# Two stacks of four heads' outputs used in turn, and the four steps that finish a stack moved to later units, in a one-core adaLN block with windowed attention

## The chip, the cores and the metric

The kernel runs on one core of a Trainium2 chip. Its time is the device time of one execution in microseconds (us); three executions were timed, and the median of the three is the metric. One more execution was profiled. Engines are named as in the profile: PE (TensorE, matmuls), PEld (its weight loads), DVE (VectorE), ACT (ScalarE), POOL (GpSimd), SP (SyncE, which issues nearly all DMAs, strictly one after the other).

## The reference

```python
h = _layernorm(x) * (1 + ca) + sa                       # x: 2048 x 448
q, k, v = split(h @ wqkv)                               # 16 heads of 28
scores = einsum("bhqd,bhkd->bhqk", q, k) * 28 ** -0.5
mask = (idx[:, None] - idx[None, :] >= 0) & (idx[:, None] - idx[None, :] < 256)
p = softmax(where(mask, scores, -1e9))
x = x + ga * (einsum("bhqk,bhkd->bhqd", p, v) @ wo)
h = _layernorm(x) * (1 + cb) + sb
x = x + gb * (mish(h @ w1 + b1) @ w2)                   # 448 -> 1792 -> 448
```

sa, ca, ga, sb, cb, gb are rows made of a condition vector; all is float32.

## The kernel before

The 2048 rows are four groups of 512 (g = 0 to 3). Each group has 16 heads, so attention is 64 heads ("slots") i = 16g + h, and each slot is three **units** u = 3i, 3i+1, 3i+2, the three blocks of keys that its 512 queries see. Matmul operands are split into a high and a low part (hi, lo) to keep the precision, which is why there are two or three matmuls for each product.

The order of the work is written out by hand in one loop over u (the loop with `for u in range(NU + 9)`). In the iteration of unit u, with s = u // 3 and k = u % 3, it records, in this order:

- `PV(u - 4, Pl)`: the low part of the probabilities of unit u-4 times the values, into the PSUM tile pv of its slot (line 750). At k = 0 also `EV(s - 2)`, which copies the finished pv of slot s-2 to the staging tile O2 (ACT, line 756).
- `B(u)`: the scores with keys on the partitions (PE, tile sB, line 718), the mask by a matmul (line 729), and two exponentials on ACT, P (line 732) and its rounded copy Ph (line 733). The row maximum is subtracted inside the matmul: two rows of the query tile q hold it.
- `SP(u - 1)`: the low piece Pl = P - Ph of the unit before (POOL, line 740, one subtraction of 128x512).
- `A(s + 3, t)`: for a slot three ahead, scores with queries on the partitions (PE, tile sA, line 688) and their row maximum with the mask (DVE, tile junk, line 690). Two PSUM buffers serve all sA.
- a load of q and k for a later slot from the scratch tensor scr (SP); then the filler of the group: matmuls of the projections qk and qk_v and of the output projection wo (line 323), as many as a credit of RATE per unit allows, with their evictions.
- `M2`: every six units the row maxima of two slots are transposed on PE (line 696), split on DVE (mr, lines 698 and 699) and sent by two small DMAs into the q tiles (q<-mr). `B` of the first of these slots, three units later, reads them.
- At k = 1 `EM(s - 2)`: two DMAs move the staged output of a slot to its place in a stack of four heads: rows 0 to 31 of the staging tile to partitions 32(i % 4) and on of tile O4 (o<-o), rows 32 to 59 to the same partitions of tile OL4 (ol<-o). O4 holds the product with the high part of the values and the row sum of the softmax, OL4 the product with the low part. `PV(u - 2, Ph)` ends the iteration.

There is one pair O4, OL4. When its four heads are in, **four steps** finish the stack of quad qd (slots 4qd to 4qd+3):

- `QA(qd)`: on = O4 + OL4, POOL, line 776;
- `T1(qd)`: a transpose by 32x32 blocks into T4 and a reciprocal of the row sums, DVE, lines 782 and 784;
- `TM(qd)`: T4 times the reciprocals, POOL, line 789;
- `T2(qd)`: the transpose back, DVE, line 793. The last quad of a group then sets `on_full`, for which that group's output projection (gen_oT and gen_wo, in the next group's filler) waits.

Before the change QA stands at the very start of unit 12qd+18, ahead of that unit's `SP`; T1 in unit 12qd+19, TM in 12qd+20, T2 in 12qd+22. The last transfer into the stack is recorded in unit 12qd+16, and the first into the same pair for the next quad in unit 12qd+19. Engines take their instructions in the recorded order, and a waiting instruction holds all that is behind it on its engine; a DMA that SP waits to issue holds the later ones. The last four slots don't use the staging tile: EV copies them straight into O4 and OL4 (lines 758 and 759), and the last quad's four steps are recorded together after the last unit. After attention (about 472 us) comes the dense part: z and acc matmuls (lines 937, 1130 to 1132).

Of the kernel before, what the change touches and what calls it, by code (L numbers as in the profile page):

```python
# [8 lines left out]
F32 = mybir.dt.float32  # L9
F32R = mybir.dt.float32r  # L10
BF16 = mybir.dt.bfloat16
AF = mybir.ActivationFunctionType
ALU = mybir.AluOpType

S, D, F, H, DH, W = 2048, 448, 1792, 16, 28, 256
NG, GT = 4, 512
# [35 lines left out]
def adaln_block(ctx: ExitStack, tc: tile.TileContext, x, wqkv, wo, w1, b1, w2, c, w_mod, out):  # L52
    nc = tc.nc
    PE, ACT, DVE, POOL = nc.tensor, nc.scalar, nc.vector, nc.gpsimd
# [3 lines left out]
    def dma(o, i):  # L58
        nc.sync.dma_start(o, i)

    def pool(name, side="left", space=None):
        kw = {} if space is None else {"space": space}
        cm = tc.tile_pool(name=name, bufs=1, reuse_waits="tile", side=side, **kw)
        st = ExitStack()
        return st.enter_context(cm), st
# [45 lines left out]
    for k in range(4):  # L111
        wmf = st0.tile([128, 2 * D], F32, name=f"wm01_{k}")
        t = wmf[0:112]
# [199 lines left out]
    def drain(*gs):  # L313
        for g in gs:
            for _ in g:
                pipe.step()
# [17 lines left out]
    def flush():  # L334
        while later:
            later.pop(0)()
# [185 lines left out]
    att, att_s = pool("att")  # L522
# [1 line left out]
    Q3 = [Q2[i // 2][:, i % 2] for i in range(NQ)]  # L524
    k3_tile(att, NK - 1)

    O4, OL4, T4, O2 = [att.tile([128, GT], F32, name=n) for n in ("o4", "ol4", "t4", "o2")]
    POOL.memset(OL4, 0.0)
    wo3 = [mid.tile([128, D], F32R, name=f"wo3_{i}", tag="wo", bufs=8) for i in range(4)]
    wol = [mid.tile([128, D], F32R, name=f"wol_{i}", tag="wo", bufs=8) for i in range(4)]  # L530

# [142 lines left out]
    NS = NG * H  # L674
    mx, Pt, Ph, Pl, pvb = {}, {}, {}, {}, {}
# [34 lines left out]
    def B(u):  # L710
        i, b = divmod(u, 3)
        g, h = divmod(i, H)
        q, k = Q3[i % NQ], K3[i % NK]
        bl = units(g, b)
        c0 = bl[0][3]
        p = bank("sB", 2, f"sB{u}")
        for n, (jj, t0, t1, c) in enumerate(by_width(bl)[::-1]):
            PE.matmul(p[:, c:c + 128 * (t1 - t0)], k[:, jj * 128:(jj + 1) * 128], q[:, t0 * 128:t1 * 128],  # L718
                      start=(n == 0), stop=False, skip_group_check=True)
        far = {c + 128 * (jj - t0) for jj, t0, t1, c in bl if t0 <= jj < t1}  # L720
        diag = {c + 128 * (jj - 2 - t0) for jj, t0, t1, c in bl if t0 <= jj - 2 < t1}
        masked = []
        for c in sorted(far | diag):
            if c in far:
                masked.append((256 if c + 128 in diag else 128, c, 0))
            elif c - 128 not in far:
                masked.append((128, c, 128))
        for n, c, m in sorted(masked):
            PE.matmul(p[:, c:c + n], identr, fdmask[:, m:m + n], start=False, stop=True, skip_group_check=True)  # L729
        P = Pt[u] = att.tile([128, 512], F32, name=f"P{u}", tag="P", bufs=4)  # L730
        Ph[u] = att.tile([128, 512], F32R, name=f"Ph{u}", tag="Ph", bufs=4)
        ACT.activation(P[:, c0:], p[:, c0:], AF.Exp, scale=SCALE)  # L732
        ACT.activation(Ph[u][:, c0:], p[:, c0:], AF.Exp, scale=SCALE)  # L733

    def SP(u):
        i, b = divmod(u, 3)
        c0 = units(i // H, b)[0][3]
        Pl[u] = att.tile([128, 512], F32R, name=f"Pl{u}", tag="Pl", bufs=4)
        for eng, a, b in ((POOL, c0, 512),) if u < NU - 5 else ((POOL, 0, 256), (DVE, 256, 512)):
            eng.tensor_tensor(Pl[u][:, a:b], Pt[u][:, a:b], Ph[u][:, a:b].bitcast(F32), op=ALU.subtract)  # L740

    def PV(u, P):
        i, b = divmod(u, 3)
        g, h = divmod(i, H)
        if P is Ph and b == 0:
            pvb[i] = bank("pv", 2, f"pv{i}")
        pv = pvb[i]
        for n, (jj, t0, t1, c) in enumerate(by_width(units(g, b))):
            j = 4 * g - 2 + jj
            PE.matmul(pv[0:60, t0 * 128:t1 * 128], V[j % NV][:, h, :], P[u][:, c:c + 128 * (t1 - t0)],  # L750
                      start=(P is Ph and b == 0 and n == 0), stop=False, skip_group_check=True)

    def EV(i):
        a, b = i % 4 * 32, i % 2 * 64
        if i < NS - 4:
            ACT.activation(O2[b:b + 60], pvb[i][0:60, :], AF.Copy)  # L756
        else:
            ACT.activation(O4[a:a + 32], pvb[i][0:32, :], AF.Copy)
            DVE.tensor_copy(OL4[a:a + DH], pvb[i][32:60, :])

    def EM(i):
        a, b = i % 4 * 32, i % 2 * 64
        if i < NS - 4:
            dma(O4[a:a + 32], O2[b:b + 32])
            dma(OL4[a:a + DH], O2[b + 32:b + 60])

    def quad(qd):
        g, ci = divmod(qd, 4)
        if ci == 0 and g not in on:
            on[g] = mid.tile([128, 4, GT], F32, name=f"on{g}", tag="on")  # L770
        return on[g][:, ci], T4.rearrange("p (b d) -> p b d", d=32)

    def QA(qd):
        o, t = quad(qd)
        for eng, a, b in ((POOL, 0, GT),) if qd < NS // 4 - 1 else ((POOL, 0, 192), (DVE, 192, GT)):
            eng.tensor_tensor(o[:, a:b], O4[:, a:b], OL4[:, a:b], op=ALU.add)

    rcq = {}

    def T1(qd):  # L780
        o, t = quad(qd)
        DVE.transpose(T4, o)
        rcq[qd] = att.tile([128, 16, 1], F32, name=f"rc{qd}", tag="rc", bufs=1)
        DVE.reciprocal(rcq[qd], t[:, :, 28:29])

    def TM(qd):
        o, t = quad(qd)
        for eng, a, b in ((POOL, 0, 16),) if qd < NS // 4 - 1 else ((POOL, 0, 6), (DVE, 6, 16)):
            eng.tensor_tensor(t[:, a:b, 0:28], t[:, a:b, 0:28], rcq[qd][:, a:b].to_broadcast([128, b - a, 28]), op=ALU.mult)

    def T2(qd):
        o, t = quad(qd)
        DVE.transpose(o, T4)
        if qd % 4 == 3:
            on_full.add(qd // 4)
# [213 lines left out]
    def step(g):  # L1009
        return next(fillers[g], 99.0) or RATE[g]  # L1010
# [40 lines left out]
    for u in range(NU + 9):  # L1051
        s, k = divmod(u, 3)
        g = s // H
        if k == 0 and s % H == 0 and 0 < g < NG:
            drain(fillers[g - 1], side[g - 1])
            flush()
        pipe.step()
        qd = (s - 6) // 4
        if s % 4 == 2 and 0 <= qd < NS // 4 - 1 and k == 0:
            QA(qd)  # L1060
        if 0 <= u - 4 < NU:
            PV(u - 4, Pl)
            if k == 0:
                EV(s - 2)
        if u < NU:
            B(u)
        if 0 <= u - 1 < NU:
            SP(u - 1)
        a = s + LEAD
        if a < NS:  # L1070
            A(a, (0, 1, 3)[k])
        if k == s % 2 and s < NS:
            load_slot(s + LEAD + 2)
        if 0 <= qd < NS // 4 - 1:
            if s % 4 == 2 and k == 1:
                T1(qd)
            if s % 4 == 2 and k == 2:
                TM(qd)
            if s % 4 == 3 and k == 1:
                T2(qd)  # L1080
        if k == 0 and s - 2 == NS - 1:
            for f in (QA, T1, TM, T2):
                f(NS // 4 - 1)
        if g < NG:
            v = u - 48 * g
            if v in (0, 12):
                chunk["v"] = 4 if v == 0 and g or 0 < g < NG - 1 else 2
            if v == 0:
                credit = 0.0
            credit += RATE[g] * (2 if v < FRONT[g] else 1)  # L1090
            while credit > 0.0:
                credit -= step(g)
        if k == 0 and (a - 1) % 2 == 1 and LEAD <= a - 1 < NS:
            M2((a - 1) // 2)
        if g < NG:
            if v > 1 or g == 0:
                side_step(g, ("dve", "act")[a >= NS:] if k == 1 else ("act",) if k == 0 and s % 2 == 0 else ())
            if later and ((s + (k == 2)) % 2 == 0 or k == 1):
# [12 lines left out]
        if 0 <= u - 2 < NU:  # L1111
            PV(u - 2, Ph)
# [53 lines left out]
    for n in range(NN + 1):  # L1166
        g, f = divmod(n, NF)
# [44 lines left out]
```

## Time and profile before

| | us |
|---|---|
| median of three timed executions (768.67, 770.18, 770.5) | 770.18 |
| the profiled execution | 768.72 |
| its span | 766.9 |
| PE busy in the span | 701.2 |
| DVE, ACT, POOL busy | 397.6, 392.1, 347.9 |
| mean granted clock of PE | 0.962 |

The span runs from the first to the last instruction of the program; the 1.8 us between it and the execution's time lie around it. A busy share is an average over stages, so what a change in attention is worth has to be read from the stretch of attention, about 59 to 472 us. PEclk is the share of the full TensorE clock that was granted: where it is 0.5, a matmul takes about twice as long. The idle time that a view puts ahead of an instruction is put down to the wait that ended last.

### The profile page before, as it was taken

What the parts mean: (1) busy time and instruction counts of PE and PEld (TensorE: products, weight loads), DVE (VectorE), ACT (ScalarE), POOL (GpSimd) and SP (SyncE); (2) the same over time, 40 slices, a digit from 0 to 9 for tenths busy, and PEclk for the clock granted to TensorE, in tenths of its full rate; (3) what the DMA queues carried; (4) which work ended last, traced back from release to release, by engine and by line L of the source; (5) the groups of instructions that cost most, each with busy time, mean ns of one, the idle gap of its engine ahead of it and who ended that gap; (6) DMA issues with size and microseconds to landing.
All of it is one profiled execution on the core that took longest, in us unless ns stands there. A gap on an engine that the chain in (4) does not pass through costs nothing.

```text
span 766.9 us, 11988 instructions
## 1 busy us (share of the span) xinstructions
PE 701.2 (91%) x3873; PEld 594.2 (77%) x3873; DVE 397.6 (52%) x993; ACT 392.1 (51%) x723; POOL 347.9 (45%) x363
## 2 busy tenths in 40 slices
PE   8999868969899979899987879999999999999996
PEld 8777656748778858787866768888888888888885
DVE  6676645667646657756575778443422232323112
ACT  4467645766746657756665679343323322322221
POOL 6545865678454678555586695642100000000002
PEclk9999998989989979999989899999999999999999
DMA  7856762364456364464667425530110020001001
GB/s 223 264 192 201 206 205 86 107 198 126 134 175 204 100 188 142 138 177 152 183 192 208 126 70 181 169 108 1 50 48 0 1 96 0 1 1 49 0 1 49
DMA packets 53730, 91.13 MB, mean 119 GB/s; under 512 B 8086, under 2 KB 28228, under 8 KB 53668
## 3 DMA queue, kind: packets, MB, share of 16 engines
q1 hardware_dynamic: 53204, 90.36, 38.5%
q8 instruction: 31, 0.51, 0.3%
q14 instruction: 31, 0.25, 0.1%
q10 hardware_dynamic: 464, 0.00, 0.0%
HBM read 53.34 MB, written 29.36 MB: 108 GB/s over the span
## 4 chain that ended last, share of the span: by engine, by line
PE 65%; issue 13%; DMA 8%; DVE 6%; POOL 3%; ACT 3%; SPq 1%; POOLq 0%; ACTq 0%; DVEq 0%
PE z L937 14%; PE pv L750 8%; PE qk L323 7%; PE wo L323 5%; PE sB L718 4%; PE acc L1132 4%; PE acc L1130 4%; PE acc L1131 4%; DMA ol<-o 4%; PE sA L688 4%; PE sB L729 3%; PE qk_v L323 2%; DVE junk L690 2%; POOL Pl L740 2%; PE warm L436 1%
## 5 line engine op out<-in xcount | busy, mean ns | idle before, releaser
L740 POOL TENSOR_TENSOR Pl<-P,Ph 128x512 fp32r<-128x512 f32 (+2 forms) x192 | 233.9, 1232 | 68.7 <-ACT Ph L733 45.9
L690 DVE CUSTOM_DVE_ANT_0 junk<-sA,mask 128x384 bf16<-128x384 f32 (+2 forms) x256 | 133.8, 523 | 93.3 <-PE sA L688 82.6
L732 ACT ACTIVATE P<-sB 128x512 f32<-128x512 f32 (+2 forms) x192 | 109.5, 570 | 81.6 <-PE sB L729 76.0
L945 DVE TENSOR_TENSOR al<-t,ah 128x512 fp32r<-128x512 f32 x56 | 40.8, 728 | 187.1 <-ACT ah L944 187.0
L943 ACT ACTIVATE t<-z,b1c 128x512 f32<-128x512 f32 x56 | 38.5, 687 | 190.0 <-PE z L937 183.2
L688 PE MATMUL sA<-k,q 84*128 84x384 f32 (+2 forms) x256 | 104.1, 416 | 7.5 <-DVE mx L690 6.2
L733 ACT ACTIVATE Ph<-sB 128x512 fp32r<-128x512 f32 (+2 forms) x192 | 109.2, 569 | 0.0
L750 PE MATMUL pv<-Pl,v 128*60 128x256 f32 (+2 forms) x352 | 79.0, 300 | 30.6 <-POOL Pl L740 30.5
L718 PE MATMUL sB<-q,k 86*128 86x256 f32 (+1 forms) x352 | 80.5, 304 | 14.2 <-DMA q<-mr 8.5
L937 PE MATMUL z<-hhf,w 128*128 128x512 f32 x224 | 89.5, 399 | 0.0
L937 PE MATMUL z<-hlf,w 128*128 128x512 f32 x224 | 88.5, 395 | 0.0
L750 PE MATMUL pv<-Ph,v 128*60 128x256 f32 (+2 forms) x352 | 82.1, 309 | 0.0
L1130 PE MATMUL acc<-w2h,ah 128*128 128x448 f32 x224 | 81.9, 366 | 0.0
L1132 PE MATMUL acc<-w2h,al 128*128 128x448 f32 x224 | 81.9, 366 | 0.0
L1131 PE MATMUL acc<-w2l,ah 128*128 128x448 f32 x224 | 81.5, 364 | 0.0
L718 PEld LDWEIGHTS sB<-q,k 86*128 86x128 f32 x352 | 65.4, 205 | 19.7 <-issue 8.8
L750 PEld LDWEIGHTS pv<-Pl,v 128*60 128x60 f32 x352 | 47.3, 141 | 42.3 <-POOL Pl L740 36.3
L937 PE MATMUL z<-hhf,w1l 128*128 128x512 f32 x168 | 66.4, 395 | 0.0
L688 PEld LDWEIGHTS sA<-k,q 84*128 84x128 f32 x256 | 51.9, 207 | 15.6 <-DVE mx L690 10.9
L729 PE MATMUL sB<-fdmask,identr 128*128 128x128 bf16 (+1 forms) x320 | 63.8, 267 | 0.0
L750 PEld LDWEIGHTS pv<-Ph,v 128*60 128x60 f32 x352 | 48.8, 142 | 13.8 <-issue 2.0
L756 ACT ACTIVATE o<-pv 60x512 f32<-60x512 f32 x60 | 35.3, 589 | 41.7 <-PE pv L750 39.2
(157 smaller groups left out, 1261.2 us busy)
## 6 DMA issues: line engine op xcount, KB each, us to landing
scr<-st SPq DMA_DIRECT2D x24, 512.0 KB
k<-scr SPq DMA_DIRECT2D x48, 252.0 KB
q<-scr SPq DMA_DIRECT2D x64, 168.0 KB
scr<-st SPq DMA_DIRECT2D x32, 256.0 KB
x<-x1d SPq DMA_DIRECT2D x10, 448.0 KB
o<-o SPq DMA_DIRECT2D x60, 64.0 KB
xin<-in_A_x_dram SPq DMA_DIRECT2D x8, 448.0 KB
xr<-in_A_x_dram SPq DMA_DIRECT2D x16, 224.0 KB
```

Of the source, the lines that this page charges most:

```text
L323: PE.matmul(p, b, a, start=(n == 0), stop=(n == len(ps) - 1))
L688: PE.matmul(p[:, c0:384], q[0:84, t * 128:(t + 1) * 128], k[0:84, t * 128 + c0:t * 128 + 384], start=True, stop=True)
L690: DVE.tensor_tensor_reduce(out=junk[:, c0:384], in0=p[:, c0:384], in1=mask[:, c0:384], scale=1.0, scalar=-3.0e38, op0=ALU.add, op1=ALU.max ...
L718: PE.matmul(p[:, c:c + 128 * (t1 - t0)], k[:, jj * 128:(jj + 1) * 128], q[:, t0 * 128:t1 * 128], start=(n == 0), stop=False, skip_group_ch ...
L732: ACT.activation(P[:, c0:], p[:, c0:], AF.Exp, scale=SCALE)
L733: ACT.activation(Ph[u][:, c0:], p[:, c0:], AF.Exp, scale=SCALE)
L740: eng.tensor_tensor(Pl[u][:, a:b], Pt[u][:, a:b], Ph[u][:, a:b].bitcast(F32), op=ALU.subtract)
L750: PE.matmul(pv[0:60, t0 * 128:t1 * 128], V[j % NV][:, h, :], P[u][:, c:c + 128 * (t1 - t0)], start=(P is Ph and b == 0 and n == 0), stop=F ...
L937: PE.matmul(zb[n], ps[m][1], ps[m][0], start=(m == 0), stop=(m == 10))
L1130: PE.matmul(p, ah[n][:, ts], w2h[f], start=(f == 0), stop=False)
L1131: PE.matmul(p, ah[n][:, ts], w2l[f], start=False, stop=False)
L1132: PE.matmul(p, al[n][:, ts], w2h[f], start=False, stop=(f == NF - 1))
```

## The change

O4 and OL4 become two pairs (two lists of two tiles); T4 and O2 keep their roles and get the names t4_0 and t4_1, so in rows of the changed program the staging tile reads "t". EV, EM and QA choose the pair by the quad's parity, i // 4 % 2. The four steps of a quad move to one unit each, in units 12qd+20 to 12qd+23, and behind that unit's `B`, `SP`, `A` and load instead of ahead of them. The last quad's steps stay where they are. One more memset clears the second OL4.

```diff
-    O4, OL4, T4, O2 = [att.tile([128, GT], F32, name=n) for n in ("o4", "ol4", "t4", "o2")]
-    POOL.memset(OL4, 0.0)
+    O4, OL4, (T4, O2) = [[att.tile([128, GT], F32, name=f"{n}_{i}") for i in range(2)] for n in ("o4", "ol4", "t4")]
+    for t in OL4:
+        POOL.memset(t, 0.0)
...
     def EM(i):
-        a, b = i % 4 * 32, i % 2 * 64
+        a, b, n = i % 4 * 32, i % 2 * 64, i // 4 % 2
         if i < NS - 4:
-            dma(O4[a:a + 32], O2[b:b + 32])
-            dma(OL4[a:a + DH], O2[b + 32:b + 60])
+            dma(O4[n][a:a + 32], O2[b:b + 32])
+            dma(OL4[n][a:a + DH], O2[b + 32:b + 60])
...
-            eng.tensor_tensor(o[:, a:b], O4[:, a:b], OL4[:, a:b], op=ALU.add)
+            eng.tensor_tensor(o[:, a:b], O4[qd % 2][:, a:b], OL4[qd % 2][:, a:b], op=ALU.add)
...
         pipe.step()
-        qd = (s - 6) // 4
-        if s % 4 == 2 and 0 <= qd < NS // 4 - 1 and k == 0:
-            QA(qd)
         if 0 <= u - 4 < NU:
             PV(u - 4, Pl)
...
         if k == s % 2 and s < NS:
             load_slot(s + LEAD + 2)
-        if 0 <= qd < NS // 4 - 1:
-            if s % 4 == 2 and k == 1:
-                T1(qd)
-            if s % 4 == 2 and k == 2:
-                TM(qd)
-            if s % 4 == 3 and k == 1:
-                T2(qd)
+        qd, w = divmod(u - 20, 12)
+        if 0 <= qd < NS // 4 - 1 and w < 4:
+            (QA, T1, TM, T2)[w](qd)
```

EV changes as EM does: for the last four slots it writes O4[n] and OL4[n].

Two places of the program's order are shown, both of quad 5 (the sixth). On POOL, the rows before (Pl are the low pieces of one unit each, on is the sum QA, t the multiplication TM):

```order
L740 TENSOR_TENSOR Pl_2694<-P_2663,Ph_2664 128x512
L776 TENSOR_TENSOR on_2358<-o_462,ol_463 128x512
L740 TENSOR_TENSOR Pl_2721<-P_2690,Ph_2691 128x512
L740 TENSOR_TENSOR Pl_2748<-P_2717,Ph_2718 128x512
L740 TENSOR_TENSOR Pl_2776<-P_2744,Ph_2745 128x512
L789 TENSOR_TENSOR t_464<-t_464,rc_2754 128x16x28
L740 TENSOR_TENSOR Pl_2803<-P_2772,Ph_2773 128x512
```

and the same stretch of POOL in the changed program (buffer numbers differ between the programs: the first three rows are the units of Pl_2721, Pl_2748 and Pl_2776 above):

```order
L741 TENSOR_TENSOR Pl_2717<-P_2691,Ph_2692 128x512
L741 TENSOR_TENSOR Pl_2742<-P_2713,Ph_2714 128x512
L741 TENSOR_TENSOR Pl_2773<-P_2738,Ph_2739 128x512
L777 TENSOR_TENSOR on_2426<-o_1_463,ol_1_465 128x512
L741 TENSOR_TENSOR Pl_2796<-P_2769,Ph_2770 128x512
L741 TENSOR_TENSOR Pl_2829<-P_2792,Ph_2793 128x512
L790 TENSOR_TENSOR t_0_466<-t_0_466,rc_2803 128x16x28
L741 TENSOR_TENSOR Pl_2911<-P_2825,Ph_2826 128x512
```

Three low pieces that stood behind the sum now stand ahead of it; between the sum and the multiplication there are two instead of three.

On DVE, before (the pairs L690 are the row maxima of one sA tile; L262 and L270 split a transposed tile; L698 and L699 make mr):

```order
L782 STREAM_TRANSPOSE t_464<-on_2358 128x512
L784 RECIPROCAL rc_2754<-t_464 128x16
L690 ISA junk,mx_2639<-sA_2_2758,mask 128x384
L690 ISA mx_2639 128x1
L262 TENSOR_SCALAR tr_2728<-tr_2728,cols 128x512
L270 TENSOR_TENSOR hl_2585<-tr_2728,hh_2584 128x512
L690 ISA junk,mx_2639<-sA_3_2778,mask 128x384
L690 ISA mx_2639 128x1
L690 ISA junk,mx_2805<-sA_0_2806,mask 128x384
L690 ISA mx_2805 128x1
L698 CAST mr_2814<-sA_3_2778 8x128
L699 TENSOR_TENSOR mr_2814<-sA_3_2778,mr_2814 8x128
```

and in the changed program:

```order
L691 ISA junk,mx_2639<-sA_3_2775,mask 128x384
L691 ISA mx_2639 128x1
L262 TENSOR_SCALAR tr_2747<-tr_2747,cols 128x512
L270 TENSOR_TENSOR hl_2611<-tr_2747,hh_2610 128x512
L691 ISA junk,mx_2798<-sA_0_2799,mask 128x384
L691 ISA mx_2798 128x1
L783 STREAM_TRANSPOSE t_0_466<-on_2426 128x512
L785 RECIPROCAL rc_2803<-t_0_466 128x16
L699 CAST mr_2811<-sA_3_2775 8x128
L700 TENSOR_TENSOR mr_2811<-sA_3_2775,mr_2811 8x128
```

The transpose T1 and its reciprocal have moved behind three row maxima and now stand directly ahead of the two instructions that make mr.

In groups 1 and 2, where the output projection waits for `on_full`, its first matmuls come one unit later and what follows them in the group's filler moves back by a unit; the order of the dense part is unchanged.

More of the change, by code (lines that the diff above doesn't have):

```diff
@@ L757, in EV @@
         else:
-            ACT.activation(O4[a:a + 32], pvb[i][0:32, :], AF.Copy)
-            DVE.tensor_copy(OL4[a:a + DH], pvb[i][32:60, :])
+            ACT.activation(O4[n][a:a + 32], pvb[i][0:32, :], AF.Copy)
+            DVE.tensor_copy(OL4[n][a:a + DH], pvb[i][32:60, :])
     def EM(i):
-        a, b = i % 4 * 32, i % 2 * 64
+        a, b, n = i % 4 * 32, i % 2 * 64, i // 4 % 2
         if i < NS - 4:
-            dma(O4[a:a + 32], O2[b:b + 32])
-            dma(OL4[a:a + DH], O2[b + 32:b + 60])
+            dma(O4[n][a:a + 32], O2[b:b + 32])
+            dma(OL4[n][a:a + DH], O2[b + 32:b + 60])
     def quad(qd):
```

## Prediction

> **What bounds the kernel now.** I read the page first, then the engines' busy time by stage, then PE's waits.
>
> ```profile
> span 766.9 us, 11988 instructions
> 59.00:160.00 101.00, 81.35 (x485) 63.95 (x484) 58.89 (x187) 60.40 (x130) 63.66 (x62) 0.95 0.53 164
> 160.00:272.00 112.00, 103.05 (x633) 87.69 (x632) 70.62 (x202) 72.41 (x135) 71.03 (x62) 0.93 0.50 150
> 272.00:385.00 113.00, 100.58 (x633) 85.78 (x633) 70.15 (x201) 72.43 (x135) 75.20 (x66) 0.95 0.55 166
> 385.00:460.00 75.00, 61.32 (x391) 50.34 (x391) 53.89 (x140) 50.04 (x96) 58.36 (x50) 0.91 0.50 146
> 460.00:767.00 307.00, 300.44 (x1418) 260.46 (x1417) 104.25 (x157) 104.10 (x168) 47.12 (x53) 0.99 0.15 47
> ```
>
> Each row is a stretch, its length, the busy time of PE, PEld, DVE, ACT and POOL, the granted clock, the DMA share and GB/s. From 460 us on PE is busy for 300.44 of 307 us; nothing here is to be had there. In the four rows of attention PE is busy for 346.3 of 401 us, so it idles 54.7 us, and no other engine comes near it: POOL, the next, has 268.3. What ends PE's waits:
>
> ```profile
> PE pv L750 <- POOL Pl L740: 30.5, 14, 4.3
> PE sB L718 <- DMA q<-mr: 8.5, 6, 3.7
> PE sA L688 <- DVE mx L690: 6.2, 12, 1.0
> PE sB L718 <- ACT Ph L733: 4.7, 5, 2.2
> ```
>
> (total us, times, longest.) More than half of the idle time is one wait: PV wants a low piece that POOL has not made. It comes 14 times, and there are 15 quads in the loop. POOL itself in attention:
>
> ```profile
> L740 POOL TENSOR_TENSOR Pl<-P,Ph 128x512 fp32r<-128x512 f32 x179 | 222.6, 1258 | 61.8 <-ACT Ph L733 40.4 <-PE sA L688 7.7 <-POOL Pl L740 4.9
> L776 POOL TENSOR_TENSOR on<-o,ol 128x512 f32<-128x512 f32 x15 | 19.1, 1273 | 70.6 <-DMA ol<-o 35.9 <-PE sA L688 18.5 <-DMA q<-scr 6.1
> L789 POOL TENSOR_TENSOR t<-t,rc 128x448 f32<-128x448 f32 x14 | 13.8, 983 | 0.0
> ```
>
> Ahead of 15 sums POOL idles 70.6 us, 4.7 us each. The views name several releasers, but the sum reads only the stack and waits for its transfers. Quad 5 shows the whole event:
>
> ```profile
> 201.18 0.28 DVE L699 TENSOR_TENSOR mr<-sA,mr 8x128 fp32r<-8x128 f32 x1
> 203.81 0.47 PE L718 MATMUL sB<-q,k 86*128 86x384 f32 x2
> 204.18 0.81 SPq L59 DMA_DIRECT2D ol<-o  x1
> 204.83 0.56 DVE L690 CUSTOM_DVE_ANT_0 junk<-sA,mask 128x384 bf16<-128x384 f32 x1
> 205.39 0.40 PE L718 MATMUL sB<-q,k 86*128 86x256 f32 x2
> 206.57 0.40 PE L718 MATMUL sB<-q,k 86*128 86x384 f32 x2
> 209.50 1.26 POOL L776 TENSOR_TENSOR on<-o,ol 128x512 f32<-128x512 f32 x1 [6.10 <-DMA ol<-o]
> 210.72 3.74 POOL L740 TENSOR_TENSOR Pl<-P,Ph 128x512 fp32r<-128x512 f32 x3
> 210.79 0.56 SPq L59 DMA_DIRECT2D o<-o  x1
> 210.80 0.71 DVE L782 STREAM_TRANSPOSE t<-on 128x512 f32<-128x512 f32 x1 [3.47 <-POOL on L776]
> 211.54 0.25 DVE L784 RECIPROCAL rc<-t 128x16 f32<-128x16 f32 x1
> 212.04 0.68 PE L750 MATMUL pv<-Pl,v 128*60 128x128 f32 x2 [3.06 <-POOL Pl L740]
> ```
>
> The last transfer is issued at 204.18 and the sum starts at 209.50, 5.3 us later. Three low pieces wait behind it, DVE's transpose waits for it (3.47 us), SP's next o<-o waits for it, and PE stands for 3.06 us. Units are 1.2 to 1.6 us long here (203.81, 205.39, 206.57).
>
> The clock follows. These stretches begin at PE's stalls behind a sum (the last one at the copy of the end of attention, below):
>
> ```profile
> 132.00:139.80 7.80, 7.07 (x36) 5.29 (x36) 6.30 (x19) 5.54 (x12) 7.80 (x8) 0.78 0.36 98
> 159.00:168.00 9.00, 7.40 (x39) 6.17 (x40) 5.36 (x18) 4.62 (x9) 8.68 (x11) 0.62 0.41 121
> 210.00:218.00 8.00, 5.96 (x23) 5.10 (x24) 4.79 (x13) 2.32 (x5) 7.83 (x7) 0.57 0.07 17
> 275.00:284.00 9.00, 7.07 (x31) 5.80 (x32) 5.17 (x18) 4.22 (x8) 8.68 (x11) 0.53 0.50 147
> 384.00:393.00 9.00, 7.08 (x31) 5.24 (x32) 5.85 (x16) 3.48 (x7) 8.54 (x8) 0.62 0.34 114
> 436.00:445.00 9.00, 7.88 (x39) 6.49 (x40) 7.62 (x20) 4.83 (x10) 8.83 (x9) 0.62 0.18 54
> 459.00:468.00 9.00, 9.00 (x53) 7.42 (x52) 7.67 (x14) 8.88 (x18) 5.55 (x7) 0.81 0.02 5
> ```
>
> Length times missing clock, summed over the seven, is 21.4 us; counting only what PE was busy, 17.6 us.
>
> **The change part by part.** The sum stood at the head of unit 12qd+18 and now comes behind the low piece of unit 12qd+19: three low pieces go ahead of it.
>
> *The low-piece waits, -30.5.* In quad 5 POOL's wait of 6.10 us is to be covered by three units, 3 x 1.5 = 4.5 us, so at most about 1.6 us of wait is left, and behind it stands a piece that PE wants only three units later. With the average wait of 4.7 us nothing is left. I take all 30.5, and give back under "new crowding" what the late cases cost.
>
> *The clock, -15.* If the stalls go, so should the half-clock stretches: 0 to 21.4. I take 17.6 less a little for stretches that other gaps will still throw low.
>
> How long a stall must be to cost clock the rows don't settle. The stall of 3.06 us that ends at 212.04 stands in a stretch with 0.57. The two longest are
>
> ```profile
> 159.74 0.68 PE L750 MATMUL pv<-Pl,v 128*60 128x128 f32 x2 [3.93 <-POOL Pl L740]
> 276.10 0.68 PE L750 MATMUL pv<-Pl,v 128*60 128x128 f32 x2 [4.26 <-POOL Pl L740]
> ```
>
> and in the rows at 159 and 275 the busy time times the missing clock is 2.8 + 3.3 = 6 us.
>
> [...]
>
> *The end of attention, -2.* The last four slots are copied straight into the stack, and the copy waits for the sum that still reads it:
>
> ```profile
> ACT o L758 <- POOL on L776: 2.0, 1, 2.0
> ```
>
> With two stacks it no longer does. ACT's exponentials stand behind it, hence PE's longest wait for Ph of 2.2.
>
> *Row maxima, -1.5.* DVE no longer sits in T1 (3.5 us in quad 5) with maxima behind it; of PE's 6.2 us for mx I take a quarter (0 to 6.2).
>
> *SP, 0.* Transfers of the next quad wait for the sum now:
>
> ```profile
> SPq L59 <- POOL on L776: 26.9, 13, 4.7
> ```
>
> 26.9 us of queue time go, and what is behind them issues earlier: the loads of q and k, and in one place a q<-mr (PE's longest such wait is 3.7). I book nothing and let the range have 0 to -3.7.
>
> *T1 ahead of mr, +9.* This is the new wait. T1 and its reciprocal, 0.71 + 0.25 = 0.96 us, stand directly ahead of CAST mr, 15 times. The chain that follows, mr, two DMAs, sB, took 2.35 us from mr's end (201.46) to sB (203.81) with nothing to spare. Quad 8 shows spare time:
>
> ```profile
> 303.61 0.28 DVE L698 CAST mr<-sA 8x128 fp32r<-8x128 f32 x1 [0.37 <-PE sA L696]
> 303.92 0.28 DVE L699 TENSOR_TENSOR mr<-sA,mr 8x128 fp32r<-8x128 f32 x1
> 307.75 0.40 PE L718 MATMUL sB<-q,k 86*128 86x384 f32 x2
> ```
>
> From 304.20 to 307.75 are 3.55 us, 1.2 more than needed, and DVE was idle for 0.37 of what T1 will take. To the 0.96 comes what T1 waits for the sum. In quad 5 the sum could end at 209.5 + 1.27 = 210.8 if its DMA lands as now; DVE gets to T1 about at sB of unit 21 (206.57 + 1.4) plus 1.6 (sB at 203.81 to the end of its maxima at 205.39), at 209.6: 1.2 us of wait, in one of the worst quads. So a quad costs between 0 (spare time 1.2, no wait) and 0.96 + 1.5 = 2.5 (none to spare): 0 to 37 in all. Most quads wait little at T1; 0.96 - 0.37 = 0.6 each is 9.
>
> *New crowding, +3.* Four units now hold four low pieces, the sum and the multiplication: 4 x 1.26 + 1.27 + 0.98 = 7.3 us of POOL against 4 x 1.4 = 5.6 of short units, 1.7 us behind; the spare of three units covers it except in late quads: 0 to 8, taken 2. In two groups the output projection starts one unit later, and a unit without filler may leave PE short by up to its length: 0 to 3, taken 1. The forced filler at the group's end does the work anyway.
>
> *At nothing:* the second memset runs while POOL waits in the first stage; uncovered it could not cost more than one sum of the same tile, 1.27. TM and T2 have the same durations as before; T2 may wait for TM, with maxima behind it that have two sA buffers of slack.
>
> Sum: -30.5 - 15 - 2 - 1.5 + 9 + 3 = -37. The profiled execution took 768.7 (span 766.9), so 731.7 by the trace; the median shown, 770.2, is 1.5 above it: 733.
>
> **The rivals.**
>
> *Little of the clock comes back.* Only the two longest stalls (3.93 and 4.26 us) had clock to lose, and the other stretches go slow for small gaps that remain. The term shrinks from 15 to 6 and the time is 733 + 9 = 742. For it: the row at 459 has 0.81 though PE is busy for all of it. Against: the other stretches, too, begin at stalls of this wait. [...]
>
> *The wait moves to q<-mr.* T1 waits 1.5 us in every quad: 0.96 - 0.37 + 1.5 less half of the 1.2 spare is 1.5, times 15 is 22 instead of 9; with gaps still there, 10 of the clock instead of 15: 733 + 13 + 5 = 751. For it: mr's wait is already PE's second longest. Against: 4.7 us of average wait meets 4.5 us or more of new distance.
>
> *Slower.* The same place, decided by one number: T1's wait. The whole gain before the mr term is 49 us less 3 of crowding, 46, or 3.1 a quad. With a spare of 0.6, the change loses once T1 waits 3.1 + 0.6 - 0.6 = 3.1 us or more, that is if transfers land about 2 us later against the units than now, because units get shorter and DMAs do not. At 4 us it is 15 x 4.0 - 46 = +14: 784. For it: DMA is busy half of the time (0.50 to 0.55) and 5.3 us from issue to sum is long. Against: quad 5's 1.2.
>
> *No change.* PE only waits for the next thing, exponentials or loads, and keeps its pace: 770. Against: ACT, at 255.3 of 401 us, has room.
>
> **How the numbers follow.** Forecast 0.66 (720 to 745), little clock 0.10 (742), wait moves 0.13 (751), same 0.04, slower 0.07. A measurement of this kernel can tell about 0.3% (2.3 us) from no change. Faster 0.89, same 0.04, slower 0.07. The range goes from 718 (all the clock, all the row maxima and the SP term: -30.5 - 21.4 - 2 - 6.2 - 3.7 + 9 + 3 = -52) to 756, which takes in the moved wait with 5 to spare.
>
> **What would show it.** Right: PE's wait for Pl under 6 us; POOL's idle ahead of the sums down from 70.6 to under 20; SP's wait for the sum gone; the granted clock of the four rows of attention up from 0.91 to 0.95 to about 0.97; PE's wait for q<-mr up from 8.5 to about 15. Wrong: waits for q<-mr of 25 us or more, DVE still waiting over 30 us at T1, or the clock rows unchanged.

## The result and the profile after

| | before | after |
|---|---|---|
| median of the timed executions, us | 770.34 (4, 768.67 to 771.94) | 742.32 (4, 740.08 to 747.59) |
| ratio of the two, 95% interval | | 0.9646 [0.9585, 0.9708] |
| the profiled execution, us | 768.7 | 740.1 |
| its span, us | 766.9 | 738.3 |
| PE busy, us | 701.2 | 690.1 |
| span less PE busy: PE's idle time, us | 65.7 | 48.2 |

The times are medians, with the number of executions and their lowest and highest in brackets. The change made the kernel 28 us faster; 37 were forecast. The span is 28.6 us shorter, and the table splits that in two: PE idles 17.5 us less and is busy for 11.1 us less. The second part is clock, since the matmuls are the same (3873 in both profiles): the mean granted clock went from 0.962 to 0.980. In the changed kernel the projection's 128x512 matmuls start 0.43 us apart from 88.21 on, where the clock is 0.50, and 0.23 us apart from 90.96 on, where it is 0.99.

PE's waits of the changed kernel in attention (total us, times, longest):

```profile
PE sB L719 <- DMA q<-mr: 13.5, 7, 5.7
PE sA L689 <- DVE mr L700: 10.5, 7, 3.0
PE sA L689 <- DVE mx L691: 8.2, 16, 1.1
PE sB L719 <- ACT Ph L734: 2.3, 3, 1.3
```

The row of before that carried the argument, PV's wait for a low piece (30.5 us), is not there at all. In its place stands a wait that before did not have: PE's scores sA wait for mr. The four stretches of attention (columns as in the prediction: stretch, length, busy time of PE, PEld, DVE, ACT, POOL, granted clock, DMA share, GB/s):

```profile
59.00:160.00 101.00, 84.40 (x502) 66.85 (x500) 62.09 (x194) 63.49 (x136) 68.62 (x69) 0.93 0.54 166
160.00:272.00 112.00, 104.66 (x664) 89.40 (x665) 75.17 (x217) 76.21 (x143) 78.16 (x70) 0.96 0.55 169
272.00:385.00 113.00, 105.69 (x690) 90.11 (x689) 77.89 (x222) 80.14 (x151) 80.49 (x65) 0.99 0.62 183
385.00:460.00 75.00, 69.35 (x430) 58.41 (x429) 59.84 (x129) 55.98 (x105) 59.98 (x53) 0.99 0.54 162
```

The clock went from 0.95, 0.93, 0.95, 0.91 to 0.93, 0.96, 0.99, 0.99: it rose in three rows and fell in the first. Length times missing clock, summed over the four rows, is 25.3 us before and 13.4 after.

POOL's groups in attention, and the waits of DVE, SP and ACT that have to do with the stacks:

```profile
L741 POOL TENSOR_TENSOR Pl<-P,Ph 128x512 fp32r<-128x512 f32 (+2 forms) x186 | 226.3, 1224 | 100.6 <-ACT Ph L734 64.1 <-PE pv L751 8.5 <-POOL Pl L741 7.9
L777 POOL TENSOR_TENSOR on<-o,ol 128x512 f32<-128x512 f32 (+1 forms) x16 | 20.3, 1270 | 8.3 <-DVE ol L760 5.0 <-PE sA L689 1.6 <-DMA o<-t 1.0
```

```profile
DVE t L783 <- POOL on L777: 6.1, 5, 2.1
...
SPq L59 <- POOL on L777: 0.4, 1, 0.4
...
ACT t L757 <- DMA ol<-t: 11.1, 8, 3.0
```

POOL idled 70.6 us ahead of its sums and now 8.3, of which 5.0 belong to the last quad, outside the loop. DVE's wait at T1 and SP's at the next transfer are all but gone. ACT's copy into the staging tile now waits more, 11.1 us.

### The profile page after: what moved, and what is told of

It is laid out like the page before. It is cut to its first block, busy times and chain, and to the rows that moved or that the text cites. A ratio compares the mean times of both kernels' runs of the same rounds, so it can differ in the third digit from the quotient of the medians.

```text
span 738.3 us, 12000 instructions
## 1 busy us (share of the span) xinstructions
PE 690.1 (93%) x3873; PEld 585.9 (79%) x3873; DVE 395.3 (54%) x993; ACT 391.5 (53%) x723; POOL 348.6 (47%) x364
## 5 line engine op out<-in xcount | busy, mean ns | idle before, releaser
L691 DVE CUSTOM_DVE_ANT_0 junk<-sA,mask 128x384 bf16<-128x384 f32 (+2 forms) x256 | 135.2, 528 | 104.2 <-PE sA L689 93.0
L689 PE MATMUL sA<-k,q 84*128 84x384 f32 (+2 forms) x256 | 103.4, 408 | 19.8 <-DVE mr L700 10.5
L719 PE MATMUL sB<-q,k 86*128 86x256 f32 (+1 forms) x352 | 77.7, 295 | 16.1 <-DMA q<-mr 13.5
L751 PE MATMUL pv<-Ph,v 128*60 128x256 f32 (+2 forms) x352 | 79.8, 302 | 0.0
L719 PEld LDWEIGHTS sB<-q,k 86*128 86x128 f32 x352 | 62.1, 195 | 21.4 <-issue 10.8
L751 PE MATMUL pv<-Pl,v 128*60 128x256 f32 (+2 forms) x352 | 75.6, 289 | 0.1
L689 PEld LDWEIGHTS sA<-k,q 84*128 84x128 f32 x256 | 50.4, 199 | 30.5 <-DVE mx L691 14.1
L730 PE MATMUL sB<-fdmask,identr 128*128 128x128 bf16 (+1 forms) x320 | 61.6, 259 | 0.0
L751 PEld LDWEIGHTS pv<-Ph,v 128*60 128x60 f32 x352 | 47.2, 137 | 12.9 <-issue 0.6
L1133 POOL TENSOR_TENSOR yo<-yo,x 128x448 f32<-128x448 f32 (+1 forms) x4 | 4.2, 1058 | 108.1 <-DVE yo L1130 108.1
```

Of the source, the lines that this page charges most:

```text
L689: PE.matmul(p[:, c0:384], q[0:84, t * 128:(t + 1) * 128], k[0:84, t * 128 + c0:t * 128 + 384], start=True, stop=True)
L691: DVE.tensor_tensor_reduce(out=junk[:, c0:384], in0=p[:, c0:384], in1=mask[:, c0:384], scale=1.0, scalar=-3.0e38, op0=ALU.add, op1=ALU.max ...
```

## The new waits, each at its place

DVE around the end of quad 3, in the changed kernel:

```profile
158.39 0.71 DVE L783 STREAM_TRANSPOSE t<-on 128x512 f32<-128x512 f32 x1 [2.11 <-POOL on L777]
159.13 0.25 DVE L785 RECIPROCAL rc<-t 128x16 f32<-128x16 f32 x1
159.30 0.21 DVE L699 CAST mr<-sA 8x128 fp32r<-8x128 f32 x1
159.55 0.28 DVE L700 TENSOR_TENSOR mr<-sA,mr 8x128 fp32r<-8x128 f32 x1
```

PE at the same time:

```profile
155.51 0.27 PE L697 MATMUL sA<-ident,mx 128*8 128x128 f32 x1
...
159.88 0.69 PE L689 MATMUL sA<-k,q 84*128 84x384 f32 x1 [2.94 <-DVE mr L700]
```

PE had transposed the row maxima by 155.8. DVE could have split them then, but T1 stands ahead and waits 2.11 us for the sum. So mr is finished at 159.8, and PE stands for 2.94 us. It does not stand at sB, which needs mr three units later. It stands at the second score tile sA behind the transposition (the first, at 156.53, still starts without a wait): the transposed maxima lie in spare columns of an sA tile, two buffers serve all sA, and a score tile that takes this buffer may not start until DVE has read them. POOL shows why the sum was late here:

```profile
152.72 0.24 POOL L233 TENSOR_SCALAR rsa<-mva 128x4 f32<-128x4 f32 x1 [0.79 <-DVE mva L220]
...
154.63 2.50 POOL L741 TENSOR_TENSOR Pl<-P,Ph 128x512 fp32r<-128x512 f32 x2
157.09 1.26 POOL L777 TENSOR_TENSOR on<-o,ol 128x512 f32<-128x512 f32 x1
```

The sum no longer waits for its transfers. It waits in POOL's row, behind two low pieces that a layer norm's small steps had held back.

The longest wait for q<-mr is another matter. SP's queue, and PE:

```profile
101.98 3.43 SPq L59 DMA_DIRECT2D wop<-in_A_wo_dram  x8
...
107.03 1.78 SPq L59 DMA_DIRECT2D wop<-in_A_wo_dram  x4
...
109.91 1.40 SPq L59 DMA_DIRECT2D q<-mr  x2
```

```profile
112.84 0.66 PE L719 MATMUL sB<-q,k 86*128 86x384 f32 x1 [5.70 <-DMA q<-mr]
```

The loads of the output weights (wop) stand ahead of the two small DMAs in SP's queue. DVE had finished mr at 104.5, and SP issues the two q<-mr only from 109.91 on; PE stands for 5.70 us. Before the change the same loads stood there too, SP issued these two at 109.77, and PE's wait was shorter:

```profile
112.60 0.66 PE L718 MATMUL sB<-q,k 86*128 86x384 f32 x1 [3.71 <-DMA q<-mr]
```

So this wait was there already. The queue has kept its pace and PE now reaches the place 1.8 us sooner.

## The experiments

The theory at the start: three low pieces ahead of the sum are the whole gain, and what is left to win is T1's place ahead of mr. The rivals: the second stack itself gives the gain, by freeing SP's queue; and what is left is no single wait, since taking one away only brings up the next. All ratios are against the kernel before.

**Two stacks, old places.** The four steps go back to their old units; the two stacks stay.

```diff
+        if s % 4 == 2 and 0 <= qd < NS // 4 - 1 and k == 0:
+            QA(qd)
...
-            (QA, T1, TM, T2)[w](qd)
+            if s % 4 == 2 and k == 1:
+                T1(qd)
```

(TM and T2 in the same way.)

> Two stacks in turn, but the four steps stay in their old places (the sum at the head of unit 12qd+18, the first transpose in 12qd+19, and so on). Theory (the gain comes from the three low pieces that go ahead of the sum; the second stack only makes it safe): the sum still stands ahead of the low pieces and still waits for the same transfers, so POOL's idle time ahead of the sums stays near 70 us and PE's wait for the low piece near 30; only SP's wait for the sum (26.9) and the copy at the end of attention (2.0) go: 763 to 769. Rival (the second stack itself is the gain, because transfers no longer queue behind a wait for the sum and so land earlier): PE's wait for the low piece falls under 15 and the time is 745 to 757.

Measured: 767.31 us (10 executions), ratio 0.9987 [0.9965, 1.0009]. PE's and SP's waits and POOL's sums in this run:

```profile
PE pv L751 <- POOL Pl L741: 30.9, 15, 4.2
```

```profile
SPq L59 <- POOL on L777: 1.4, 3, 0.7
```

```profile
L777 POOL TENSOR_TENSOR on<-o,ol 128x512 f32<-128x512 f32 x14 | 17.8, 1274 | 68.3 <-DMA ol<-t 16.2 <-DMA o<-t 12.3 <-ACT P L733 8.1
```

SP's wait for the sum falls from 26.9 to 1.4 us and buys nothing that can be measured. SP is not free for it: in attention its wait for mr rises from 76.5 to 104.2 us, and all its waits together stay at 181 to 183. POOL and PE wait as before. So the gain needs the later place; the second stack alone does not give it. With one pair the sum could not stand in unit 12qd+20, because the next quad's first transfer, recorded in unit 12qd+19, would overwrite what it has still to read. That follows from the recorded order; no kernel with one pair and a later sum was run.

**T1 behind mr.** T1 alone is recorded behind M2 in its unit, so that mr no longer stands behind it.

```diff
-        if 0 <= qd < NS // 4 - 1 and w < 4:
+        if 0 <= qd < NS // 4 - 1 and w in (0, 2, 3):
             (QA, T1, TM, T2)[w](qd)
...
             M2((a - 1) // 2)
+        if 0 <= qd < NS // 4 - 1 and w == 1:
+            T1(qd)
```

> The changed kernel with one step moved: the first transpose and its reciprocal are recorded behind M2 of the same unit, so DVE makes mr first. Theory (a part of the gain was given back because mr stands behind the transpose on DVE, and PE then waits for mr at the next sA tile that uses the bank in which the transposed maxima stand): PE's wait of sA for mr falls from 10.5 to under 2, its wait for q<-mr from 13.5 to about 10, and the clock comes back with it: 730 to 737. Rival (the transpose only shows a lateness of POOL and of transfers; the wait goes on at the next place): 739 to 745.

Measured: 744.41 us (4), 0.9708 [0.9662, 0.9753], no gain over the changed kernel. PE's waits:

```profile
PE sA L689 <- DVE mx L691: 19.4, 23, 4.3
PE sB L719 <- DMA q<-mr: 10.2, 6, 5.8
```

The wait for mr (10.5) is gone, and the wait for row maxima has grown from 8.2 to 19.4. Its longest, 4.3 us, ends at 167.75 and has a cause that can be seen. On DVE the subtraction hlo (the low part of a finished stack, for the output projection) stands ahead of the row maxima:

```profile
161.10 6.12 DVE L632 TENSOR_TENSOR hlo<-on,hho 128x512 fp32r<-128x512 f32 x1
...
168.33 0.69 DVE L632 TENSOR_TENSOR hlo<-on,hho 128x512 fp32r<-128x512 f32 x1
```

and POOL over the same time:

```profile
159.95 2.52 POOL L741 TENSOR_TENSOR Pl<-P,Ph 128x512 fp32r<-128x512 f32 x2
162.42 0.23 POOL L223 COPY xin<-xin 128x64 f32<-128x64 f32 x1
162.61 2.48 POOL L741 TENSOR_TENSOR Pl<-P,Ph 128x512 fp32r<-128x512 f32 x2
165.05 0.23 POOL L223 COPY xin<-xin 128x64 f32<-128x64 f32 x1
165.24 1.26 POOL L741 TENSOR_TENSOR Pl<-P,Ph 128x512 fp32r<-128x512 f32 x1
166.45 0.23 POOL L223 COPY xin<-xin 128x64 f32<-128x64 f32 x1
```

The same subtraction takes 0.69 us once and 6.12 us the other time: it ends at 167.22, 0.54 us after POOL's unbroken row of instructions. It looks as if DVE did not get its turn between POOL's instructions; that is the author's reading of these rows, and no run shows what holds the subtraction up.

**mr into another bank.** The transposed maxima go to the bank of the newest sA tile.

```diff
-            M2((a - 1) // 2)
+            M2((a - 1) // 2, "A")
```

> The changed kernel, but the maxima are transposed into the spare columns of the newest sA bank instead of the one before it, so that not the next sA tile but the one after it needs mr to be done; DVE's order is unchanged. Theory (the wait goes through the bank): PE's wait of sA for mr falls from 10.5 to under 3 and q<-mr stays at 12 to 15: 732 to 738. Rival (mr's lateness is what costs, on whichever way): what sA no longer waits sB waits for q<-mr, which rises by 6 to 10, and the time is 740 to 745.

Measured: 745.48 us (4), 0.9704 [0.966, 0.9749]. PE's waits:

```profile
PE sA L697 <- DVE mx L691: 13.5, 16, 2.0
PE sB L719 <- DMA q<-mr: 12.4, 8, 5.8
PE sA L689 <- DVE mr L700: 6.4, 4, 2.4
```

The wait for mr falls to 6.4, and the transposition itself now waits 13.5.

**All four steps one unit earlier.**

```diff
-        qd, w = divmod(u - 20, 12)
+        qd, w = divmod(u - 19, 12)
```

> The changed kernel with all four steps one unit earlier (units 12qd+19 to 12qd+22), so that two low pieces instead of three go ahead of the sum and the first transpose is not directly ahead of mr any more (a row maximum stands between them). Theory (two units cover most of the transfers' time, and the place ahead of mr is what costs): POOL's idle time ahead of the sums rises from 8.3 to 15 to 30, PE's wait for the low piece from 0 to 2 to 6, its wait of sA for mr falls under 5: 737 to 745, within 1% of the changed kernel. Rival (the distance is everything, each unit of it is worth a third of the gain): 748 to 756.

Measured: 743.56 us (4), 0.9682 [0.9649, 0.9715]. PE does not wait for a low piece here either, and the wait for mr is gone. Two low pieces ahead of the sum are already enough, though POOL idles 18.1 us ahead of its sums instead of 8.3 and DVE waits 12.0 us at T1 instead of 6.1. The wait for row maxima is 15.3 us instead of 8.2. In this place the sum is recorded ahead of the next quad's first transfer, so one pair of stacks might do; that was not run.

**Two units for each step**, so that no step waits for the one before.

```diff
-        if 0 <= qd < NS // 4 - 1 and w < 4:
-            (QA, T1, TM, T2)[w](qd)
+        if 0 <= qd < NS // 4 - 1 and w in (0, 2, 4, 6):
+            (QA, T1, TM, T2)[w // 2](qd)
```

> The changed kernel with two units between the four steps instead of one (units 12qd+20, +22, +24, +26): the first transpose stands a unit behind mr, and DVE should never wait for the sum. Theory (DVE's wait for the sum and its place at mr are what costs): DVE's wait at the first transpose falls from 6.1 to under 1, PE's waits for DVE (mr and mx together, 18.7 in the changed kernel) to under 9: 730 to 736. Rival (at the new pace DVE has no slack in the short units, wherever the turnings stand): PE's waits for DVE stay at 14 to 20 and the time at 738 to 746.

Measured: 747.05 us (4), 0.9715 [0.968, 0.975]: DVE waits only 2.3 us at T1, and the time is the longest of the variants, though its interval overlaps that of the change. PE waits for low pieces again (3.3 us in all), and the granted clock of the four stretches is 0.95, 0.95, 0.94 and 0.91. Why was not tried.

**A second staging tile**, against ACT's new wait of 11.1 us.

```diff
-            ACT.activation(O2[b:b + 60], pvb[i][0:60, :], AF.Copy)
+            ACT.activation(O2[i // 2 % 2][b:b + 60], pvb[i][0:60, :], AF.Copy)
```

(The two transfers read the same tile.)

> The changed kernel with four staging areas for the slots' outputs instead of two, so that ACT's copy of a finished pv waits for the transfers of four slots ago and not of two. ACT's wait for these transfers rose from 2.1 to 11.1 with the change. Theory (it lies on PE's path through the exponentials behind it): the wait goes and the time falls by 3 to 7, to 735 to 739. Rival (ACT has slack, the low pieces and PE never notice): ACT's wait goes, the time stays at 741 to 745.

Measured: 742.18 us (4), 0.9651 [0.9616, 0.9686]. ACT's wait is gone and the time is the same: it cost nothing.

**T1 reads another tile**, so that it never waits for the sum; it still stands ahead of mr. This kernel leaves the sum out of its result.

```diff
-        DVE.transpose(T4, o)
+        DVE.transpose(T4, o if qd == NS // 4 - 1 else other)
```

> The changed kernel, but the first transpose of the quads in the loop reads a constant tile instead of the sum, so it has the same length and place on DVE and never waits for POOL (the sum is left out of the result). Theory (the wait of DVE at the first transpose costs): PE's waits for DVE fall from 18.7 to under 10, and the time by 6 to 10, to 732 to 737. Rival (DVE's own load at this place costs, not its wait): they stay at 14 to 18, and the time at 739 to 744.

Measured: 743.84 us (4), 0.9661 [0.9615, 0.9706]. The wait for mr falls from 10.5 to 4.5, that for row maxima grows from 8.2 to 14.2; the stretched subtraction is back, with 6.11 and 3.15 us. Without T1's wait for the sum the kernel is not faster; how much the stretched subtraction hides here is open.

**T1 behind mr, and the output projection's first step a unit later**, to take the subtraction away from POOL's row.

```diff
     def gen_oT(g, oT_pool):
+        yield
```

> The kernel with the first transpose behind mr (744.4), and the split of the finished stacks for the output projection one unit later. There one subtraction hlo on DVE took 6.1 us and one 3.3 instead of 0.7 while POOL worked without a pause. Theory (DVE's operations with two SBUF inputs can't start while POOL's stand back to back, and this hid the gain of moving the transpose): no hlo over 1.5 us, PE's wait for mx falls from 19.4 to under 13, 736 to 741. Rival (a chance event of that run, or one that returns elsewhere): 743 to 747.

Measured: 745.43 us (4), 0.9703 [0.9657, 0.9748]. No subtraction takes over 1.7 us any more, the wait for row maxima is 13.7 us instead of 19.4, and the time did not fall. That it is the two SBUF inputs that hold the subtraction up, as the theory has it, no run shows.

**T1 behind mr, and the subtraction on POOL.**

```diff
-            pipe.add(2, None, lambda ci=ci: DVE.tensor_tensor(ol[:, ci], o[:, ci], oh[:, ci].bitcast(F32), op=ALU.subtract))
+            pipe.add(2, None, lambda ci=ci: POOL.tensor_tensor(ol[:, ci], o[:, ci], oh[:, ci].bitcast(F32), op=ALU.subtract))
```

> The kernel with the first transpose behind mr (744.4), whose two stretched subtractions hlo on DVE (6.1 and 3.3 us) are now done by POOL itself. Theory (DVE could not start them while POOL's operations stood back to back): no operation of DVE is stretched there, PE's wait for mx falls from 19.4 to 12 to 15, and the time to 738 to 742. Rival (PE's wait for mx has other causes): it stays over 17 and the time at 743 to 748.

Measured: 743.71 us (6), 0.9689 [0.9659, 0.9718]. The wait for row maxima is 12.7 us, no subtraction is left on DVE to be stretched, and the time did not fall: the same answer in another way.

**The output weights issued by ACT instead of SP.**

```diff
-                dma(t[32 * a:32 * a + DH], wo[r:r + DH, :])
+                nc.scalar.dma_start(t[32 * a:32 * a + DH], wo[r:r + DH, :])
```

> The changed kernel, with the 16 small loads of the output projection's weights (wop) issued by ACT instead of SP. In its trace a q<-mr whose data was ready at 104.5 is issued at 109.9, behind twelve of these loads and other transfers, and PE waits 5.7 us with 6.8 us at half clock after it. Theory (what is left of PE's waits are transfers held up on SP and in the queue, which the shorter units uncover): PE's wait for q<-mr falls from 13.5 to 7 to 9, the clock there stays whole: 734 to 738. Rival (waits only change places, as in the experiments on DVE): another wait takes it up, ACT's for instance, and the time is 740 to 745.

It was run beside the changed kernel once more, on the same chip:

> The changed kernel as it is, so that the small differences of the experiments are read against it on one chip: 740 to 744, and the same waits as in its first profile.

Measured: 741.63 us (6), 0.9655 [0.963, 0.968]; the changed kernel 743.74 us (5), 0.9684 [0.9662, 0.9706]. The intervals overlap. PE's waits with ACT's issues:

```profile
PE sB L719 <- DMA q<-mr: 8.6, 9, 2.9
...
PE sB L719 <- ACT Ph L734: 5.5, 5, 3.1
```

The wait for q<-mr is 8.6 us, against 16.3 in the changed kernel's second profile, and its longest 2.9 instead of 5.8: the loads in SP's queue were the cause of the long one. Part of it comes back as a wait for ACT, which now issues them.

**All together:** T1 behind mr, the projection a unit later, the weights from ACT.

> The two moves that took a wait of PE away, together: the first transpose behind mr with the split for the output projection one unit later (745.4 against before's 769), and the wop loads issued by ACT (741.6). Theory (the waits are separate and their removal adds up): no wait of sA for mr, q<-mr at 7 to 9, PE's idle time in attention under 30 and the time 735 to 738. Rival (at this pace one wait takes the place of another, all engines and transfers being near their limit in the short units): idle time stays at 33 to 38, and the time at 739 to 744, no better than the wop loads alone.

Measured: 742.8 us (6, 736.68 to 747.2), 0.9654 [0.9607, 0.9702]: not better than the change alone. PE's waits:

```profile
PE sA L690 <- DVE mx L692: 13.9, 21, 1.9
PE sB L720 <- ACT Ph L735: 5.0, 6, 2.3
PE sB L720 <- DMA q<-mr: 4.3, 6, 1.7
```

Here the waits did go. The sum of PE's idle time, 739.7 less 700.1 busy, is 39.6 us, 8.6 less than in the changed kernel. But PE is busy for 10.0 us more, and the clock says why: it is 0.90, 0.95, 0.97 and 0.98 in the four stretches of attention, lower in all four than after the change (0.93, 0.96, 0.99, 0.99). Length times missing clock is 20.6 us against 13.4.

Two profiles do not show that this belongs to the kernels, though. The mean clock of every execution is on record: 0.971 to 0.981 in the six of this kernel, 0.974 on average, and 0.971 to 0.980 in the nine of the changed kernel (both series), 0.976 on average. The profiles compared here have 0.971 and 0.980, the one at the low end and the other at the high end; the execution of this kernel with 0.981 was its fastest, 736.68 us. The averages are 0.002 apart, about 1.5 us of 740. As far as six and nine executions tell, most of the 10.0 us is a difference between executions.

## Idle time and clock together

Each row is one profiled execution. Idle is the span less PE's busy time; missing clock is length times (1 - granted clock) over the four stretches of attention, worked out as above.

| kernel | execution, us | PE idle | missing clock | both |
|---|---|---|---|---|
| before | 768.7 | 65.7 | 25.3 | 91.0 |
| two stacks, old places | 765.5 | 62.3 | 28.2 | 90.5 |
| the change | 740.1 | 48.2 | 13.4 | 61.6 |
| the change, second profile | 743.7 | 49.2 | 15.3 | 64.5 |
| a second staging tile | 740.6 | 50.6 | 10.4 | 61.0 |
| weights from ACT | 741.2 | 45.0 | 17.3 | 62.3 |
| one unit earlier | 742.5 | 45.0 | 18.6 | 63.6 |
| T1 behind mr | 741.8 | 46.4 | 18.7 | 65.1 |
| T1 behind mr, projection later | 742.4 | 46.2 | 16.7 | 62.9 |
| T1 behind mr, subtraction on POOL | 743.2 | 48.4 | 17.9 | 66.3 |
| mr into another bank | 745.8 | 52.8 | 13.8 | 66.6 |
| T1 reads another tile | 743.9 | 51.8 | 15.3 | 67.1 |
| two units each | 747.1 | 48.6 | 24.2 | 72.8 |
| all together | 741.5 | 39.6 | 20.6 | 60.2 |

The execution's time less "both" is between 674 and 681 us in every row, so these two terms are most of the 28 us; the 7 us of spread are as wide as the differences among the variants. Among these, less of the one often stands beside more of the other: "all together" idles 8.6 us less than the change and misses 7.2 us more clock; the second staging tile idles 2.4 more and misses 3.0 less. The two profiles of the same kernel differ by 1.0 and 1.9, but the mean clocks of its nine executions, 0.971 to 0.980, span 6.7 us of a 740 us execution. So the 7.2 is no more than chance can give, and a trade is not shown.

How can the clock cost the same when a stall is shorter, and differ when nothing in the kernel does? Two half-clock stretches of the change, and then one of "all together":

```profile
110.70:117.50 6.80, 4.66 (x17) 3.85 (x18) 0.74 (x5) 2.05 (x5) 1.73 (x2) 0.50 0.71 229
...
158.50:165.30 6.80, 5.42 (x24) 4.72 (x25) 4.29 (x14) 3.00 (x6) 5.89 (x6) 0.50 0.48 135
```

```profile
106.30:113.10 6.80, 5.76 (x22) 4.34 (x22) 3.28 (x10) 4.74 (x11) 4.98 (x6) 0.50 0.66 204
```

The stall of 5.70 us in the changed kernel has a stretch of 6.8 us at half clock, which begins inside it. In "all together" the stalls at this place are 2.34 and 1.04 us,

```profile
105.44 0.39 PE L720 MATMUL sB<-q,k 86*128 86x256 f32 x1 [2.34 <-ACT Ph L735]
...
108.48 0.80 PE L720 MATMUL sB<-q,k 86*128 86x384 f32 x2 [1.04 <-ACT Ph L735]
```

and the stretch is 6.8 us again: 2.3 us of idle time saved, no clock. So the shorter stalls did not lower the clock's cost here.

Whether a place costs clock at all differs between two executions of one kernel. In the changed kernel's first profile eight one-column matmuls (mc) run at 345.70, and the next two matmuls take 0.45 us, with a granted clock of 1.00 from 345.7 to 349.1:

```profile
345.70 0.93 PE L179 MATMUL mc<-ones,wm 112*128 112x1 f32 x8
346.57 0.45 PE L751 MATMUL pv<-Ph,v 128*60 128x128 f32 x2
```

In its second profile the next two matmuls behind the same eight take 0.68 us, and no wait on record ahead of them, from 341 on, is longer than 0.46 us:

```profile
347.28 0.93 PE L179 MATMUL mc<-ones,wm 112*128 112x1 f32 x8
348.14 0.68 PE L751 MATMUL pv<-Ph,v 128*60 128x128 f32 x2
```

"All together" has a half-clock stretch behind the same eight, 3.4 us with 0.50 from 345.30 on, and there these two matmuls take 0.68 us as well. What decides whether such a place costs clock was not settled.

## Why the prediction was right or wrong, point by point

The direction and the place were right, and the time lies in the range: 742.3 measured, 733.0 forecast, 718 to 756 given. The gain was 28 us of the 37. The terms, each by the profiled executions:

- **Low-piece waits, -30.5 forecast: -30.5.** The wait is gone, and the run with the old places shows that the later place did it.
- **Clock, -15: -11.1** (PE busy 701.2 to 690.1). Smaller, since half-clock stretches begin at the new stalls too, as at 158.50: three of the four rows rose, the first fell. By the mean clock of each execution (0.971 to 0.980 in nine) this term moves by several us from one to the next.
- **End of attention, -2: about -2.4** (PE's wait for Ph, 4.7 to 2.3). ACT's copies of the last slots no longer wait for the sum.
- **Row maxima, -1.5: +2.0** (6.2 to 8.2). Wrong in sign: DVE still sits at T1 for 6.1 us; what else made this wait longer was not tried.
- **SP, 0 (range 0 to -3.7): +5.0, in PE's waits for q<-mr** (8.5 to 13.5). Here the sum failed most among the waits. SP's wait of 26.9 us went, and the run with two stacks alone shows that this by itself was worth nothing. But the waits for q<-mr, which were to shrink here if anything, grew: 3.71 to 5.70 behind the wop loads, where SP issues them when it did before and PE comes sooner, and 1.18 to 3.02 at about 86. This is not T1's doing: with T1 behind mr the two are 5.84 and 2.70.
- **T1 ahead of mr, +9: +10.5** (sA's wait for mr, 0 to 10.5). The size is near, by luck: the path was another one. The working followed mr only to its DMAs and to sB, three units later, and took 0.6 us in each of 15 quads. The wait stands at a nearer place, at the scores that want the sA buffer with the transposed maxima. It comes in 7 quads, up to 2.96 us, and the 1.2 us of spare time from quad 8 did not apply to it.
- **New crowding, +3: nothing to be seen.** No low piece is waited for.

The rows add up: -30.5 - 2.4 + 2.0 + 10.5 + 5.0 and -2.1 for one wait of before that is not in the profile after (b1t for xr) make -17.5, which is PE's idle time (65.7 to 48.2); with -11.1 of clock it is the span's -28.6. Against the forecast -37 there are 5.0 for q<-mr that the sum did not have, 1.5 more at T1, 3.9 less of the clock and 3.5 at the row maxima; from these go the 3 of crowding that did not come and 2.5 of the two small rows (end of attention 0.4, b1t 2.1). That is the missing 8.4.

The rival *little of the clock comes back* gave 742, the time that was measured, but not for its reason: it wanted the clock term at 6, and it was 11.1. It let only the two longest stalls, of 3.93 and 4.26 us, cost clock; in the changed kernel shorter ones stand at half-clock stretches: the stretch at 158.50, with 0.50, begins inside the stall of 2.94 us, and one at 383.80 follows a stall of 2.40 us that ends at 383.55. *The wait moves to q<-mr* named a wait that grew, but T1 was not the cause, and T1 waited for the sum only 5 times, 6.1 us in all, where 1.5 us in every quad were supposed. *Slower* needed 3.1 us at every T1, and the longest was 2.1. *No change* is what two stacks alone give.

The theory after the result, that T1's place ahead of mr is what keeps the kernel from 730, fell: eight kernels take that wait away or shorten it and none is clearly faster. In most of these runs another wait grew as that one went, each seen in one profile; why the 8.6 us of idle time that "all together" saves in its profile do not show in its median stays open. No version beat the changed kernel clearly.

## What to carry to other kernels

The addition that waited for a DMA in POOL's row held everything behind it: POOL idled 70.6 us ahead of its sums, and PE waited 30.5 us for low pieces. Put such a step behind the work that others want soon, and spend the second buffer if the later place takes one. The buffer by itself was worth nothing here. Before a step is moved ahead of another, look up every reader of what that other one makes or frees, the next owner of its PSUM bank among them, not only the reader that is named in the code. And when a stall is shortened, read the busy time of PE together with its idle time, and the clock of several executions: in nine of the changed kernel it went from 0.971 to 0.980, about 6.7 us of 740, as much as a small gain.

## What the runs showed of the hardware

- **Half-clock stretches of 3.4 and 6.8 us, also at stalls of 2.40 to 3.02 us.** The changed kernel's first profile has six in attention, each with a granted clock of 0.50 or 0.51: four of 3.4 us and two of 6.8. Four of the six start at 86.8, 110.7, 134.6 and 158.5, 23.9 us apart each time; why so, no run shows. The stretch at 158.5 begins inside a stall of 2.94 us, 1.4 us before its end. Those at 86.8 and 383.8 begin 0.9 and 0.25 us behind the ends of stalls of 3.02 and 2.40 us.
- **A DVE subtraction of two SBUF tiles took 6.12 us instead of 0.69** while POOL ran eight instructions without a gap. Its mean in attention rose from 0.95 us in the changed kernel to 1.68 in that one.
- **A wait taken from a queue can come back in the same queue:** SP's wait for the sum fell by 25 us and its wait for mr rose by 28, with the time at 0.9987 [0.9965, 1.0009].
